# Narrower unused products in front of a retention, and one more unit's rows turned by VectorE

## The chip, the cores and the metric
The kernel runs on one core of one Trainium2 chip. The time is that of one execution on the device in microseconds (us), as the median of several runs. A profile is one execution, recorded by the hardware; its span goes from the first to the last instruction of the program and is a little shorter than the time of the same execution.

## The reference
Two stages follow each other. The first is a retention over 4 batches, 8 heads, 768 tokens and 64 features, a decaying sum over earlier tokens; the second sends every token to one of 8 experts and runs that expert's two products.

```
for t in range(S):
    state = gamma * state + k[:, :, t] (outer) v[:, :, t]
    y[:, :, t] = scale * q[:, :, t] . state
x = y, as 3072 tokens of 512 features
logits = x @ w_gate                       # 8 experts
in falling order of logits: token -> expert, at most 384 tokens each
out[tokens of e] = relu(x[tokens of e] @ w1[e]) @ w2[e]
```

The second stage can only begin when the logits of all tokens are known, since the assignment goes over all of them in falling order.

## The kernel before
The retention works on 24 units, one for each batch and each chunk of 128 tokens (unit u is batch u % 4, chunk u // 4). For a unit, TensorE makes the scores (line 409), VectorE multiplies them by a table of decays (line 412), TensorE multiplies them by the values (line 466), adds what the state gives (line 445) and adds to the state (line 481); ScalarE copies the result to the tile ys. After each chunk, `gate` makes the logits of its four units (line 562) and VectorE turns them. Units 0 to 3 are groups of their own, the others go in pairs; the last group is units 22 and 23. The order of TensorE, SyncE (SP), VectorE and ScalarE is written out by hand and is the order of the code.

In front of the retention and within its first steps stand products that nobody reads: `busy` (line 425) multiplies a tile of zeros by a tile of zeros, 12 times before the tables of decays, 8 times after them and 4 times after the first unit's scores. Each is 256 columns wide, and each makes two TensorE records, a weight load and a product.

The result of a unit has the tokens along the columns, and the second stage gathers rows of x from DRAM (the tensor xs). So every unit is turned, in one of two ways. Units 0 to 16 (`TURNED = 17`) are turned by VectorE in blocks of 32 x 32 (`block_rows`, line 510, into tiles x2 and x1) and written by four transfers on SP's queue for each unit or pair of units (`send`, line 526). Units 17 to 23 are left for the end: a generator, `rows_left`, turns one after the other by TensorE against an identity, two transposes for each half step (line 492), ScalarE copies the unit to xr (lines 502 and 504) and SP writes it by one transfer (line 506). The generator is advanced once, then three times, around the last gate and the last counts:

```
        while len(written) < TURNED:
            block_rows(len(written))
        for i in range(B * LONG, TURNED):
            send_one(i)
...
        rows = rows_left(left_over)
        next(rows)
...
        for _ in range(3):
            next(rows)
```

and then, with `STEPS = 7, 3, 0`, seven and three times between steps of `search`, which finds the tokens of the first expert: counts of tokens over a grid of thresholds (TensorE) are compared (VectorE, tile sg), spread over all partitions by a product with ones (TensorE, psm), and reduced (VectorE, nmb); this happens twice for the first expert, and the choice of the expert, the slots and the row numbers (idx) follow from it. A small memset on GpSimd (POOL, line 1267) waits until all rows of x are in DRAM; after it POOL issues the gathers of x (line 1118). The calls of the generator beyond its end do nothing.

The results ys of units before `TURNED` share 9 buffers; those of later units have a tile each. Tile x1, for units from 16 to `TURNED` - 1, has `TURNED` - 16 buffers.

Of the kernel before, what the change touches and what calls it, by code (L numbers as in the profile page):

```python
# [37 lines left out]
TURN = 42  # L38
QUIET = 2
PRESS = 16  # L40
WARM = (12, 8, 4)
PARTS = 3
KNOWN = 3
ROWBUFS = 5
LONG = 4
TURNED = 17
GUESS = 4
WINDOW = 6
ABOVE = 4
# [20 lines left out]
def tile_retention_moe(ctx: ExitStack, tc: tile.TileContext, qkv, wg, w1, w2,  # L70
# [74 lines left out]
    class Clock:  # L145

        pe = dve = pool = dma = 0
        busy, kept = [], []
# [133 lines left out]
    def prep_tiles():  # L282
        return (sw.tile([128, COLS], F32, name="m", bufs=2), sw.tile([128, COLS], BF, name="a", bufs=2),
                sw.tile([128, COLS, E], BF, name="oh", bufs=2),
                sw.tile([128, COLS, 64], BF, name="cmp", bufs=2))
# [93 lines left out]
    def decays():  # L379

        for s in range(2):
            ps = bank()
            nc.tensor.matmul(ps.rearrange("p a b -> p (a b)"), dp[:, s, 0:C], dp[:, s, C:], start=True, stop=True)
            nc.vector.tensor_tensor(dm[:, s], ps, up[:, None, :].to_broadcast([128, HP, C]), op=OP.mult)
        ps = bank()
        nc.tensor.matmul(ps.rearrange("p a b -> p (a b)"), qp[:, 0:128], qp[:, 128:], start=True, stop=True)
        nc.scalar.activation(qtb, ps, AF.Copy)

    def bank():
        return rp.tile([128, HP, C], F32, name="sc", bufs=4)  # L390
# [6 lines left out]
    def scores(us):  # L397

        c = units[us[0]][1]
        for u in us:  # L400
            if u == B + 1:
                gate(0)()
                states([B])
            k_, q_ = LD[u][:, 0], LD[u][:, 1]
            sc = [bank() for _ in range(2)]
            for pr in range(HP):
                for s in range(2):
                    r, w = slice(64 * s, 64 * s + 64), slice(pr * C, pr * C + C)
                    nc.tensor.matmul(sc[s][:, pr, :], k_[r, w], q_[r, w], start=True, stop=True)  # L409
            am = rw.tile([128, 2, HP, C], F32, name="am", bufs=4)  # L410
            for s in range(2):
                masked.append(nc.vector.tensor_tensor(am[:, s], sc[s], dm[:, s], op=OP.mult))  # L412
            qs = ks = None
            if c:
                qs = rw.tile([128, HP, C], F32, name="qs", bufs=4)
                if u == B:
                    ks = grown(u, c)
                scaled = nc.gpsimd.tensor_tensor(qs, q_.rearrange("p (a b) -> p a b", a=HP), qtb, op=OP.mult)
                if u == nu - 1:
                    gone.append(scaled)  # L420
            if c < NC - 1 and ks is None:
                ks = grown(u, c)
            st[u] = am, qs, ks

    def busy(k, o):
        for _ in range(k):
            nc.tensor.matmul(o, warm[:, 0:128], warm[:, 0:o.shape[1]], start=True, stop=True, skip_group_check=True)  # L427
# [3 lines left out]
    def outputs(us):  # L431

        c = units[us[0]][1]
        halved = us[-1] == nu - 1
        for u in us:
            yps[u] = [rp.tile([128, HP, C], F32, name="yp", bufs=2)]
        for u in us:
            yps[u] += [bank() if halved else yps[u][0]]
        if c:
            for pr in range(HP):  # L440
                for u in us:
                    b = units[u][0]
                    for s in range(2):
                        o = 64 * (s ^ b % 2)
                        nc.tensor.matmul(yps[u][pr // 2][o:o + 64, pr, :], T[b // 2][64 * s:64 * s + 64, b % 2, pr, :],  # L445
                                         st[u][1][64 * s:64 * s + 64, pr, :],
                                         start=(pr == 0 or halved and pr == 2), stop=False, skip_group_check=True)
# [4 lines left out]
    def mix(us):  # L452
# [3 lines left out]
        for u in us:  # L456
            b = units[u][0]
            YS[b, c] = (yk.tile([128, HP, C], F32, name=f"ys{b}_{c}") if b + B * c >= TURNED else
                        yk.tile([128, HP, C], F32, name="ys", bufs=9))
# [50 lines left out]
    def block_rows(i):  # L510
# [6 lines left out]
        else:  # L517
            x = x1[i] = rw.tile([128, 4, HP, 32], F32, name="x1", bufs=TURNED - B * LONG)
        nc.vector.transpose(x.rearrange("p t d r -> p d t r"), YS[b, c].rearrange("p d (t r) -> p d t r", t=4))
# [14 lines left out]
    def go(sends, k=None):  # L534
        for _ in sends:
            k = k and k - 1
            if k == 0:
                break
# [34 lines left out]
    st = {}  # L573

    wp = rp.tile([128, 512], F32, name="sc", bufs=4)
    busy(WARM[0], wp[:, 0:256])
    m0, a0, oh0, cmp0 = prep_tiles()
    parts, whole, ended, th0, turned = None, [], None, None, None
    groups = [[u] for u in range(B)] + [[u, u + 1] for u in range(B, nu, 2)]
# [46 lines left out]

    with tc.manual_schedule(engines={nc.vector.engine, nc.scalar.engine}):
        decays()
        busy(WARM[1], wp[:, 0:256])
        scores([0])  # L630
        for g, us in enumerate(groups):
            ahead = groups[g + 1] if g + 1 < len(groups) else ()
            if not g:
                busy(WARM[2], bank()[:, 0:2].rearrange("p a b -> p (a b)"))
            if g == LATER[-1] + 1:
                outputs(us)
                scores(ahead[:1])
                mix(us[:1])
                scores(ahead[1:])
            elif ahead and g not in LATER:  # L640
                scores(ahead)
            while spare:
                load(spare.pop(), masked[-4])
                if g >= EARLY:
                    go(sent, 6)
            if g == B:
                ended = 0
            if g != LATER[-1] + 1:
                outputs(us)
            if g > B:  # L650
                aside()
            if g == len(groups) - 1:
                mix(us)
            else:
                for u in us:
                    if u in yps:
                        mix([u])
                    if u == us[0] and g == len(groups) - 2:
                        guess()
                    if u != B:  # L660
                        states([u])
            if g == len(groups) - 2:
                guessed()
            if ahead and g in LATER:
                scores(ahead)
            for i, u in enumerate(us):
                if u + DEEP < nu:
                    if i and g >= EVEN:
                        spare.append(u + DEEP)
                    else:  # L670
                        load(u + DEEP)
                        if g >= EARLY:
                            go(sent, 5)
            if g > B:
                b1, c1 = units[groups[g - 1][-1]]
                if b1 == B - 1:
                    turned, ended = gate(c1), c1
            for k in range(BLOCKS.get(g, 0)):
                if k == 2 and turned:
                    turned = turned() and None  # L680
                block_rows(len(written))
            if turned:
                turned = turned() and None
            if g > B:
                next(chosen, None)
            if g == SEND:
                go(sent)
                go(send_two(2))
        last = gate(NC - 1)
        pc = rp.tile([128, 2 * E], F32, name="sc", bufs=4)  # L690
        early = [b * NC + c for c in (0, 2) for b in range(B)]
        for k, c in enumerate(early):
            by_two(pc, cmp0, oh0, c, k == 0, k == len(early) - 1)
# [4 lines that stand above are left out]
        left_over = [lambda i: rp.tile([128, DM], F32, name="yp", bufs=2)]  # L698
        rows = rows_left(left_over)
        next(rows)  # L700
        c = NC - 1
        last()
        cols = slice(c, COLS, NC)
        f = best(L[:, :, c], cols, m0, oh0)
        reach(cols, B, m0, cmp0, th0)
        f()
        n0 = other_half(pc, nc.vector)
        far = steps_above(m0)
        next(far)
        for _ in range(3):  # L710
            next(rows)
        for k in (NC - 2, c):
            for b in range(B):
                te.matmul(pc[0:64, 0:E], cmp0[:, b * NC + k, :], oh0[:, b * NC + k, :], start=False, stop=True,
                          skip_group_check=True)
        full(pc, n0, sgs[0])
        next(far)
        codes(cols, oh0, a0)
# [833 lines left out]
```

## Time and profile before

| | |
|---|---|
| median of 3 runs | 396.56 us (396.11 to 398.07) |
| the profiled execution | 396.47 us, its span 394.6 us |
| TensorE products (PE) | busy 385.6 us, 98% of the span |
| TensorE weight loads (PEld) | 337.4 us, 85% |
| VectorE (DVE) | 263.8 us, 67% |
| ScalarE (ACT) | 155.5 us, 39% |
| GpSimd (POOL) | 146.6 us, 37% |

Times in the rows are us from the start of the span unless they are marked ns; the first number of a row of the timeline is a start, the second the time from there to the end of the last of its instructions. PE are products and PEld weight loads, which overlap them. In brackets stands how long the engine was idle before the first of them and what ended that; "issue" means that it waited for nothing that the profile shows. A product's time goes on after the next one has started.

### The profile page before, as it was taken

What the parts mean: (1) busy time and instruction counts of PE and PEld (TensorE: products, weight loads), DVE (VectorE), ACT (ScalarE), POOL (GpSimd) and SP (SyncE); (2) the same over time, 40 slices, a digit from 0 to 9 for tenths busy, and PEclk for the clock granted to TensorE, in tenths of its full rate; (3) what the DMA queues carried; (4) which work ended last, traced back from release to release, by engine and by line L of the source; (5) the groups of instructions that cost most, each with busy time, mean ns of one, the idle gap of its engine ahead of it and who ended that gap; (6) DMA issues with size and microseconds to landing.
All of it is one profiled execution on the core that took longest, in us unless ns stands there. A gap on an engine that the chain in (4) does not pass through costs nothing.

```text
span 394.6 us, 8484 instructions
## 1 busy us (share of the span) xinstructions
PE 385.6 (98%) x3454; PEld 337.4 (85%) x3456; DVE 263.8 (67%) x639; ACT 155.5 (39%) x282; POOL 146.6 (37%) x166
## 2 busy tenths in 40 slices
PE   8999999998999999999999999999999999999994
PEld 5899999884998899789988987897799889889983
DVE  1449878977998588759868776787687167156300
ACT  1332324242661364056234524343363265156210
POOL 4489693204311620451253332153264137021011
PEclk9999999999999999999999999999999999999998
DMA  7999999948642662392385491365157215710001
GB/s 308 422 417 419 409 352 318 259 120 292 220 149 108 215 243 86 102 321 81 112 260 215 143 339 53 138 218 209 50 173 277 110 54 195 311 55 27 2 27 60
DMA packets 22862, 77.64 MB, mean 197 GB/s; under 512 B 2684, under 2 KB 11644, under 8 KB 16160
## 3 DMA queue, kind: packets, MB, share of 16 engines
q0 software_dynamic: 8448, 46.14, 33.2%
q1 hardware_dynamic: 14368, 30.88, 21.5%
q8 instruction: 29, 0.48, 0.5%
q14 instruction: 17, 0.14, 0.1%
HBM read 64.43 MB, written 12.58 MB: 195 GB/s over the span
## 4 chain that ended last, share of the span: by engine, by line
PE 78%; issue 12%; DVE 2%; POOL 2%; DMA 2%; ACT 1%; POOLq 1%; another core or an unknown queue 0%; ACTq 0%; DVEq 0%
PE py L1220 26%; PE ph L1181 25%; PE sc L409 7%; PE yp L466 6%; PE yp L445 3%; PE TP L481 2%; PE pt L1131 2%; PE psm L169 2%; PE sc L562 2%; PE sc L427 1%; DMA xg<-xs,idx 1%; POOL wraw L1071 1%; DMA out<-yo,oix 1%; POOL out L1201 1%; PE ph L1160 1%
## 5 line engine op out<-in xcount | busy, mean ns | idle before, releaser
L1181 PE MATMUL ph<-xh,w1h 128*128 128x384 f32 x248 | 81.7, 343 | 0.0
L1181 PE MATMUL ph<-xlo,w1h 128*128 128x384 f32 x256 | 81.6, 335 | 0.0
L1181 PE MATMUL ph<-xh,w1l 128*128 128x384 f32 x256 | 81.4, 335 | 0.0
L1220 PE MATMUL py<-w2h,hh 128*128 128x512 f32 x184 | 75.3, 409 | 0.0
L1220 PE MATMUL py<-w2h,hl 128*128 128x512 f32 x184 | 72.1, 392 | 0.0
L1220 PE MATMUL py<-w2l,hh 128*128 128x512 f32 x184 | 72.1, 392 | 0.0
L1201 POOL DMA_INDIRECT out<-yo,oix x23 | 27.9, 1214 | 105.5 <-ACT yo L1197 98.9
L1071 POOL DMA_INDIRECT wraw<-w,wix x32 | 38.3, 1197 | 58.1 <-DVE un L169 44.0
L1186 ACT ACTIVATE hh<-ph 128x384 fp32r<-128x384 f32 x64 | 31.4, 490 | 62.2 <-PE ph L1181 61.6
L169 DVE TENSOR_TENSOR w1l<-wraw,w1h 128x1024 fp32r<-128x1024 f32 (+1 forms) x36 | 39.2, 1101 | 14.4 <-ACT w1h L1104 14.4
L169 DVE SCALAR_TENSOR_TENSOR hl<-ph,hh 128x384 fp32r<-128x384 f32 x64 | 34.8, 553 | 19.3 <-ACT hh L1186 18.8
L1181 PEld LDWEIGHTS ph<-xlo,w1h 128*128 128x128 f32 x256 | 47.7, 188 | 0.0
L1181 PEld LDWEIGHTS ph<-xh,w1l 128*128 128x128 f32 x256 | 47.6, 188 | 0.0
L1181 PEld LDWEIGHTS ph<-xh,w1h 128*128 128x128 f32 x248 | 46.4, 188 | 1.1 <-ACT xh L1136 0.4
L1118 POOL DMA_INDIRECT xg<-xs,idx x24 | 28.7, 1194 | 40.1 <-issue 31.0
L1220 PEld LDWEIGHTS py<-w2h,hl 128*128 128x128 f32 x184 | 34.5, 188 | 7.5
L412 DVE TENSOR_TENSOR am<-sc,dm 128x512 f32<-128x512 f32 x48 | 30.0, 682 | 15.8 <-PE sc L409 15.8
L169 DVE TENSOR_TENSOR w2l<-wraw,w2h 128x1024 fp32r<-128x1024 f32 x32 | 38.6, 1218 | 2.3 <-ACT w2h L1104 2.3
L1220 PEld LDWEIGHTS py<-w2l,hh 128*128 128x128 f32 x184 | 34.7, 188 | 6.2 <-DVE w2l L169 0.6
L1220 PEld LDWEIGHTS py<-w2h,hh 128*128 128x128 f32 x184 | 34.7, 188 | 5.6
L1197 ACT ACTIVATE yo<-py 128x512 f32<-128x512 f32 x23 | 13.8, 598 | 58.6 <-PE py L1220 43.4
L1104 ACT ACTIVATE w1h<-wraw 128x1024 fp32r<-128x1024 f32 (+1 forms) x36 | 33.6, 957 | 6.1 <-DMA wraw<-w,wix 5.9
(194 smaller groups left out, 546.3 us busy)
## 6 DMA issues: line engine op xcount, KB each, us to landing
ld<-qkv SPq DMA_DIRECT2D x20, 1024.0 KB, 12.9
xs<-x SPq DMA_DIRECT2D x32, 128.0 KB, 5.0
ld<-qkv SPq DMA_DIRECT2D x4, 768.0 KB, 6.5
xs<-xr SPq DMA_DIRECT2D x7, 256.0 KB, 2.2
wraw<-w,wix POOLq DMA_INDIRECT x32, 6.8
xg<-xs,idx POOLq DMA_INDIRECT x24, 3.7
out<-yo,oix POOLq DMA_INDIRECT x23, 3.1
xs<-x SPq DMA_DIRECT2D x4, 64.0 KB, 2.3
```

What stands on the lines that cost most here:

```text
L169: return f(o, *a, **k)
L409: nc.tensor.matmul(sc[s][:, pr, :], k_[r, w], q_[r, w], start=True, stop=True)
L412: masked.append(nc.vector.tensor_tensor(am[:, s], sc[s], dm[:, s], op=OP.mult))
L466: nc.tensor.matmul(yp[o:o + 64, pr, :], values(u)[:, 2 * pr + s, :], st[u][0][:, s, pr, :], start=(not c and pr == 0), stop=(pr == p[1] - ...
L1071: nc.gpsimd.indirect_dma_start(out=t, out_offset=None, in_=w1v if nm == "w1" else w2v, in_offset=bass.IndirectOffsetOnAxis(ap=wix[:, hf:hf ...
L1104: nc.scalar.activation(p[0], p[2], AF.Copy)
L1118: nc.gpsimd.indirect_dma_start(out=t, out_offset=None, in_=xs, in_offset=bass.IndirectOffsetOnAxis(ap=found[n][0][:, j:j + 1], axis=0))
L1181: nc.tensor.matmul(ph, a[:, o:o + 128], x_[:, d], start=(k == 0 and not begun), stop=(k == len(prods) - 1), skip_group_check=begun)
L1186: nc.scalar.activation(hh[:, f], ph, AF.Relu)
L1197: nc.scalar.activation(yo, py, AF.Copy)
L1201: sct = nc.gpsimd.indirect_dma_start(out=out, out_offset=bass.IndirectOffsetOnAxis(ap=oix[:, j:j + 1], axis=0), in_=yo, in_offset=None, bo ...
L1220: nc.tensor.matmul(py, h_[:, f, t], a[:, o:o + DM], start=(k == 0), stop=(k == 23))
```

## The change
The three groups of unused products become 64 products of 48 columns, 32 of 64 and 16 of 64, in the same places, and `TURNED` goes from 17 to 18: unit 17 is turned by VectorE right after the groups' loop, by the `while` loop quoted above, and sent by four transfers behind those of unit 16; the generator begins with unit 18. Unit 17's result moves from a tile of its own to the 9 shared buffers, and x1 has two buffers. `STEPS` stays.

```diff
-WARM = (12, 8, 4)
+WARM = (64, 32, 16)
...
-TURNED = 17
+TURNED = 18
...
-    busy(WARM[0], wp[:, 0:256])
+    busy(WARM[0], wp[:, 0:48])
...
-        busy(WARM[1], wp[:, 0:256])
+        busy(WARM[1], wp[:, 0:64])
...
-                busy(WARM[2], bank()[:, 0:2].rearrange("p a b -> p (a b)"))
+                busy(WARM[2], bank()[:, 0, 0:64])
```

## Rows read from the trace of the kernel before

**Rows 1.** Windows: stage, its us, busy us and instructions per engine, PEclk, DMA, GB/s.
```profile
20.00:88.00 68.00, 67.54 (x1464) 61.49 (x1461) 54.76 (x135) 23.78 (x67) 39.37 (x35) 1.00 0.93 328
...
104.00:389.00 285.00, 284.73 (x1651) 251.81 (x1651) 188.92 (x442) 119.18 (x190) 91.08 (x98) 1.00 0.43 152
```

**Rows 2.** Timeline of all engines, front: start, us, engine, line, instruction, count, idle before.
```profile
1.12 2.74 PE L427 MATMUL sc<-warm 128*128 128x256 bf16 x12 [1.12 <-DVE warm L350]
...
3.79 0.13 PEld L383 LDWEIGHTS <-am 36*128 36x128 bf16 x2 [0.41 <-DMA am<-dparts]
...
5.30 1.89 PE L427 MATMUL sc<-warm 128*128 128x256 bf16 x8
...
7.24 2.08 PE L409 MATMUL sc<-ld 64*128 64x128 f32 x16
...
9.25 1.04 PE L427 MATMUL sc<-warm 128*128 128x256 bf16 x4
...
10.35 1.16 PE L409 MATMUL sc<-ld 64*128 64x128 f32 x16
```

**Rows 3.** Line 427, the unused products: ns of one instruction, min/median/max, first and last start.
```profile
L427 PEld LDWEIGHTS <-warm x24: 102/151/152, 1.1 to 9.7; 128*128 128x128 bf16 x24
```

**Rows 4.** Timeline, the early counts of the search.
```profile
84.70 0.36 PE L169 MATMUL sc<-oh,cmp 128*128 128x16 bf16 x8
```

**Rows 5.** Timeline, weight loads of one unit's products with the values.
```profile
70.72 0.85 PEld L466 LDWEIGHTS yp<-am,ld 128*64 128x64 f32 x15
...
72.02 0.13 PEld L466 LDWEIGHTS yp<-am,ld 128*64 128x64 f32 x1 [0.46 <-issue]
```

**Rows 6.** The page: engines' busy time and instructions, and the queue of instructions.
```profile
PE 385.6 (98%) x3454; PEld 337.4 (85%) x3456; DVE 263.8 (67%) x639; ACT 155.5 (39%) x282; POOL 146.6 (37%) x166
...
q8 instruction: 29, 0.48, 0.5%
```

**Rows 7.** Windows, the stretch that ends at the gap; columns as in rows 1.
```profile
67.20:72.02 4.82, 4.61 (x93) 3.87 (x81) 4.42 (x11) 0.51 (x2) 1.63 (x2) 1.00 1.01 350
```

**Rows 8.** Timeline, VectorE around the last logits.
```profile
83.67 0.41 DVE L169 TENSOR_TENSOR cmp<-m,th 128x256 bf16<-128x256 f32 x1
...
84.80 0.32 DVE L564 STREAM_TRANSPOSE L<-sc 128x128 f32<-128x128 f32 x1 [0.72 <-PE sc L562]
```

**Rows 9.** Line 519, the block transposes: ns of one, min/median/max.
```profile
L519 DVE STREAM_TRANSPOSE x<-ys x17: 656/673/702, 30.3 to 82.0; 128x512 f32<-128x512 f32 x17
```

**Rows 10.** Timeline, the first expert's search: sg, its spreading product, transposes of rows.
```profile
86.37 0.16 DVE L169 SCALAR_TENSOR_TENSOR sg<-sc,ng 64x8 bf16<-64x8 f32 x1
...
86.58 0.17 PE L169 MATMUL psm<-sg,onesb 128*128 128x8 bf16 x1 [0.25 <-DVE sg L169]
...
88.79 0.44 PE L492 MATMUL ph<-ident,ys 128*128 128x128 f32 x2
88.90 0.16 DVE L169 SCALAR_TENSOR_TENSOR sg<-psm,ng 64x8 bf16<-64x8 f32 x1
...
89.07 0.60 PE L492 MATMUL py<-ident,ys 128*128 128x128 f32 x4
...
89.50 0.17 PE L169 MATMUL psm<-sg,onesb 128*128 128x8 bf16 x1
```

**Rows 11.** Timeline, SP's transfers of x, and POOL before the first gather.
```profile
78.02 7.38 SPq L526 DMA_DIRECT2D xs<-x  x6
...
86.27 4.54 SPq L506 DMA_DIRECT2D xs<-xr  x7
...
93.25 0.09 POOL L1267 MEMSET spacer<- 1x1 f32 x1 [0.80 <-PE pt L169]
...
94.49 0.95 POOL L1118 DMA_INDIRECT xg<-xs,idx  x1 [1.16 <-DVE idx L169]
```

**Rows 12.** Line 526, the sends: ns that one takes SP, min/median/max.
```profile
L526 SPq DMA_DIRECT2D xs<-x x36: 303/476/1571, 50.0 to 84.9; - x36
```

## The prediction
> **What bounds the kernel now.** I read three views in this order: the busy times by stage, the order of instructions at both ends of the retention, and the idle times before single instructions. By stage, TensorE has work for 67.54 of the 68.00 us between 20 and 88 us and for 284.73 of the 285.00 us from 104 us on [rows 1]. So nothing but TensorE's own order sets the time there, except on the short bridge between them, 88 to 104 us, where a chain of small VectorE and TensorE steps finds the first expert's tokens. A microsecond taken off the front, out of the retention, or off that bridge therefore comes off the end one for one, and a change to VectorE, ScalarE or a queue elsewhere is worth nothing. The change touches exactly these three places, so I cost each by itself.
>
> **The front.** Here the reader is to see how long the unused products last and what waits behind them. Twelve of 256 columns take 2.74 us and eight take 1.89 us [rows 2], so four more cost 0.85 us, 212 ns each, which is 256 columns at 1.2 GHz. The granted-clock column reads 1.00 in the stages [rows 1], but this front runs at the lower level: sixteen score products take 2.08 us at 7.24 us and 1.16 us at 10.35 us [rows 2], so the clock rises between those two groups. The change keeps the columns (12 x 256 = 64 x 48, 8 x 256 = 32 x 64, 4 x 256 = 16 x 64) and cuts them into 88 more products, each a weight load and a product: 176 records. If columns are what they cost, a pair of 48 columns takes 40 ns and one of 64 takes 53 ns, and the three stretches stay as long as they are. What could be dearer is the pair itself. The trace has no narrow pair at the lower clock. The nearest row is eight pairs of 16 columns with the same 128 x 128 bf16 weights, 0.36 us [rows 4]; one alone takes 0.17 us [rows 10], so seven more cost 0.19 us, 27 ns each at 2.4 GHz and, if all of it goes with the clock, 54 ns at 1.2 GHz. That is the upper bound: 64 x 54 = 3.5 us from 1.12 us on, an end at 4.6 us where the decay products' first weight load now starts at 3.79 us, when their table has landed (it waited 0.41 us for that transfer [rows 2]). That would be 0.8 us late, of which some 0.3 us comes back because less work is left for the lower clock; the two 64-column stretches stay at 53 ns. So 0 to 0.5 us; I take 0, because at 212 ns the weight load of a product is wholly hidden behind the one before it, and 40 ns is still more than the 27 ns that a load and a product need together where their cost is seen.
>
> The Trainium skill, "TensorE: Matmul & The Clock Gate", section "LDWEIGHTS (loading the stationary operand)", has a rule against this: a weight load takes its number of columns over 1.2, which for 128 columns is an estimate of 107 ns, and then 64 + 32 + 16 narrow products would last some 6.9 us longer than now. The row of eight pairs in 0.36 us [rows 4] contradicts it for these weights, at the higher clock.
>
> **The retention.** At 72.02 us a weight load that waits for nothing starts after 0.46 us of idle time ended by "issue", in the middle of sixteen equal products of which fifteen have just gone through in one run [rows 5]. Nothing else stops TensorE like that between 20 and 88 us (0.46 us is about all that is missing there, 68.00 - 67.54 [rows 1]). What it lacked can only be its next instruction. Instructions come by their own queue, 29 packets and 0.48 MB, 16.6 KB each; TensorE alone has 3454 + 3456 records [rows 6], so if all the packets were its own, one would hold some 240 of them, and the gap looks like the place where a packet came late, while the DMA engines were busy for a share of 1.01 of the time before it [rows 7]. With 176 records more in front, the same packet boundary falls 176 records earlier: the stretch from 67.20 to 72.02 us holds 93 + 81 = 174 of them [rows 7], so near 67 us, and the next one some 60 records (240 - 176) later than the old place. Bounds: the gap vanishes, -0.46 us, or one like it arises at another boundary, 0. A third case, two gaps, would be +0.46. I take -0.40: between 20 and 88 us there are 1464 + 1461 records [rows 1], some twelve boundaries with one gap, so a shifted row of boundaries has most likely none (and 0.06 us of the idle time may be something else).
>
> The Trainium skill, "Runtime: NRT & Kernel Launch", section "Instruction fetch mechanics", says that instructions arrive in blocks of 256, the next block while the current one executes, so that crossing into one is mostly hidden. By that the shift would be worth nothing and the sum would be 0.40 us higher; the gap at 72.02 us says that here one crossing was not hidden.
>
> **The bridge.** What is removed: unit 17's four transposes on TensorE, its two copies on ScalarE and one 256 KB transfer. What is added: one 32 x 32 block transpose on VectorE and four transfers of 64 KB on SP's queue.
> VectorE: the block transpose takes 0.67 us in the median of seventeen (0.70 at most) [rows 9]. It comes after the compare that ends at 83.67 + 0.41 = 84.08 us and before the transpose of the last logits at 84.80 us, before which VectorE now sits idle for 0.72 us waiting for TensorE's gate products [rows 8]. It fits: 0 to 0.05 us late; without that cover it would cost its 0.70 us. I take 0.02, and drop it in rounding.
> TensorE: the row generator is called 1 + 3 times, then 7 and 3 times between steps of the search. Seven units need fourteen half-steps of two transposes, six need twelve. Up to the second step eleven calls are made in both kernels, so nothing changes there; in the three calls after it the old kernel still has three halves (2 + 4 transposes at 88.79 and 89.07 us) and the new one has one. Behind them waits the product that spreads the count: VectorE's sg is ready at 88.90 + 0.16 = 89.06 us, yet the product starts at 89.50 us [rows 10]. The same hand-over one stage earlier takes 0.05 us, from 86.37 + 0.16 = 86.53 to 86.58 us [rows 10]. So the product can start at about 89.12 us: -0.38 us. Bounds: -0.39 (sg + 0.05) and 0 (some other wait is just behind). From there to the first gather everything hangs on this product (VectorE's next reduction, the choice of expert, the slots, the indices), so what is late next is only the xs rows.
> SP: its sends end at 78.02 + 7.38 = 85.40 us, the seven row transfers are issued from 86.27 to 90.81 us [rows 11]. Four sends at 0.476 us (median [rows 12]) hold SP until some 87.3 us, so the first of the six row transfers is issued about 1 us later than the first of the seven now; SP catches up, because it takes the rows at ScalarE's pace (4.54 / 7 = 0.65 us each [rows 11]) and the last now comes one such step earlier. POOL's little memset, which waits for all rows to have landed, runs at 93.25 us, and then POOL idles 1.16 us until the indices come at 94.49 us [rows 11]. If the rows came more than 1.16 us late they would decide. I take 0.
>
> **Sum.** 396.47 (the profiled execution: a span of 394.6 and 1.9 around it) + 0 (front) - 0.40 (gap) - 0.38 (bridge) = 395.7 us. That execution is 0.09 us below the median of the three runs shown, so I say 395.8 us for a median. Half a per cent is 2.0 us, about what a measurement of this kernel can tell from no change.
>
> **Rivals.**
> (a) The gap stays or finds another boundary: only the bridge counts, 396.1 us. For it: the DMA engines' share is 0.93 over the whole stretch from 20 to 88 us [rows 1], so other boundaries meet traffic as dense as this one. Chance 0.25. (The section of the Trainium skill named above comes to the same time, by another way: no crossing costs anything, so none can be saved.)
> (b) Slower: the narrow products are bound by the pair, not by columns. Place: the 64 products from 1.12 us. The point from which it decides: with p ns a pair the decays start 64p - 2670 ns late; about half is given back by the rising clock, and above 53 ns the other 48 products add p - 53 each. At 60 ns this is (1.17 + 0.34) / 2 = 0.75 us, which cancels the gain; at 75 ns (2.13 + 1.06) / 2 = 1.6 us, so 397.3 us. For it: a weight load of the unused products lasts 151 ns in the median [rows 3]; against it: those loads are hidden now, and 27 ns for a whole pair is seen at the other level. Chance 0.10.
> (c) More products in the same columns bring the higher clock earlier. The first sixteen scores would take 1.16 instead of 2.08 us and the four products before the second group 0.5 instead of 1.04 us [rows 2]: -1.4 us, 394.3 us. Chance 0.07. The reverse, the second group of scores at the lower clock too (+0.92 us) and about as much again for the rest of its unit, gives 397.6 us, and with the next unit more; chance 0.05.
> (d) The block transpose or the rows of x become the wait in front of the first gather, and the bridge gains nothing: 396.1 us or a little more. Chance 0.03.
> The forecast itself, both gains within 0.3 us: 0.50.
>
> **Numbers.** Forecast and (a) lie between 395.4 and 396.5 us and hold 0.75; with (d) and about half of (b) the range to 397.3 us holds over 0.8. I set the lower end at 394.6 us, for the case that the clock rises a part of that stretch earlier. Faster by over 0.5% (below 394.6) is (c): 0.08. Slower by over 0.5% (above 398.5) is its reverse and the far end of (b): 0.05. The rest, 0.87, can hardly be told from no change.
>
> **What the changed profile would show.** Front: 64 products in about 2.7 us from 1.12 us, the second scores still near 10.35 us. Retention: no idle weight load ended by "issue" near 72 us, or a new one elsewhere. Bridge: a block transpose just ahead of the last logits, the spreading product some 0.05 us after sg, the first gather of x about 0.8 us earlier. I would be wrong if the scores start later than 10.9 us, if the gap is merely elsewhere, or if the product behind sg still waits.

## The result and the profile after

The changed kernel takes 400.26 us (median of 6 runs, 399.56 to 400.58) where the kernel before, on the same chip, takes 397.5 us (6 runs). The ratio is 1.0058, 95% interval 1.0032 to 1.0083: slower by 2.3 us going by the ratio and by 2.8 us going by the medians, where 395.8 us and no measurable difference were forecast. (This ratio and those of the experiments are estimates over all runs; they are not the quotients of the two medians.) The profiled execution took 400.49 us, its span is 398.8 us.

First the retention, by windows of the changed kernel (columns as in rows 1). The first row is the stretch of [rows 1]; the other four run from one stall, found below, to the next.

```profile
20.00:88.00 68.00, 66.29 (x1432) 59.64 (x1429) 54.22 (x126) 21.60 (x59) 39.22 (x34) 1.00 0.94 324
33.48:45.76 12.27, 12.27 (x252) 10.79 (x251) 10.46 (x20) 2.33 (x7) 10.06 (x10) 1.00 1.01 417
45.76:57.90 12.14, 11.74 (x254) 10.91 (x253) 9.29 (x18) 4.50 (x12) 8.79 (x8) 1.00 0.98 340
57.90:69.44 11.54, 11.28 (x253) 10.16 (x253) 9.40 (x21) 4.50 (x12) 5.93 (x5) 1.00 0.99 291
69.44:76.26 6.82, 6.33 (x126) 5.69 (x126) 6.07 (x16) 1.20 (x3) 1.93 (x3) 1.00 0.97 303
```

Before, 0.46 us of TensorE's time was missing between 20 and 88 us [rows 1]; now it is 68.00 - 66.29 = 1.71 us. In that stretch 32 products fewer have started. The granted clock is 1.00 in both.

Where it is missing shows in the timeline of TensorE's weight loads. Five times a load that waits for no other engine starts late ("issue"); such a late start in the middle of equal work is called a stall here:

```profile
33.49 1.52 PEld L409 LDWEIGHTS sc<-ld 64*128 64x128 f32 x25 [0.74 <-issue]
...
45.76 0.74 PEld L466 LDWEIGHTS yp<-am,ld 128*64 128x64 f32 x13 [0.21 <-issue]
...
57.91 0.18 PEld L409 LDWEIGHTS sc<-ld 64*128 64x128 f32 x1 [0.61 <-issue]
...
69.45 0.15 PEld L562 LDWEIGHTS sc<-ys,wgf 128*32 128x32 f32 x5 [0.53 <-issue]
...
76.27 0.36 PEld L481 LDWEIGHTS TP<-ld 128*64 128x64 f32 x9 [0.63 <-issue]
```

They are of one kind with the gap of [rows 5], and they sit in the middle of equal work, as that one did. (Idle times of 0.17 to 0.20 us also stand at some first loads of a batch of products in both kernels, and are not meant.) The windows tell the spacing: from one to the next TensorE starts 252 + 251 = 503, 507, 506 and 252 weight loads and products. That is two blocks, two, two and one of some 252. Before 33.49 us the trace holds 601 products, 602 loads and 13 semaphore instructions, 1216 in all; counted in this way, every stall named here and in the experiments stands in front of record 193 + 256 n, and the gap of before in front of record 2753 = 193 + 256 x 10. So the blocks hold 256 instructions of TensorE, and they are the packets of the instruction queue: queue q8 moves packets of 16 KB, and from 20 to 88 us one of them starts between each two neighbouring records of this series. The first record of a block is called a boundary below.

The five idle times add up to 2.72 us. The early counts of the search started at 84.70 us [rows 4]; in a second profile of before (experiment 8) at 84.56 us; here at 87.32 us, 2.76 us after the latter. That the two sums agree so closely is partly chance. Set product by product against that second profile, the changed kernel falls back by 0.7, 0.2, 0.7, 0.5 and 0.7 us at the five places and hardly anywhere else, until it is 3.3 us behind; near 79 us, where the kernel before waits for VectorE for 0.29 us (line 616), 0.6 us of it come back. So the retention's loss is the stalls.

The front of the changed kernel, TensorE's timeline:

```profile
1.12 2.74 PE L427 MATMUL sc<-warm 128*128 128x48 bf16 x64 [1.12 <-DVE warm L350]
...
5.30 1.89 PE L427 MATMUL sc<-warm 128*128 128x64 bf16 x32
7.24 1.85 PE L409 MATMUL sc<-ld 64*128 64x128 f32 x16
9.02 0.64 PE L427 MATMUL sc<-warm 128*128 128x64 bf16 x16
9.59 1.28 PE L409 MATMUL sc<-ld 64*128 64x128 f32 x16
```

64 products of 48 columns last the same 2.74 us as twelve of 256, 32 of 64 the same 1.89 us [rows 2]: columns set the time. Here the clock rose within the first scores (1.85 instead of 2.08 us), so the second scores begin 0.76 us earlier than in [rows 2]. That moment moves by itself: with the same front, experiment 1 had its sixteen 64-column products in 1.04 us, all at the lower level, and a second profile of before had its second scores at 9.90 us. It is worth little here, since the third unit's scores then wait for their load (0.4 us in this profile, 1.1 us in a second one of this kernel); they start at 12.59 us, where the second profile of before has them at 12.48 us.

The bridge, all engines:

```profile
86.62 0.70 DVE L519 STREAM_TRANSPOSE x<-ys 128x512 f32<-128x512 f32 x1
87.32 0.36 PE L169 MATMUL sc<-oh,cmp 128*128 128x16 bf16 x8
87.42 0.32 DVE L564 STREAM_TRANSPOSE L<-sc 128x128 f32<-128x128 f32 x1
...
90.64 3.21 SPq L506 DMA_DIRECT2D xs<-xr  x6
...
91.52 0.16 DVE L169 SCALAR_TENSOR_TENSOR sg<-psm,ng 64x8 bf16<-64x8 f32 x1
...
91.73 0.17 PE L169 MATMUL psm<-sg,onesb 128*128 128x8 bf16 x1
...
97.41 0.09 POOL L1267 MEMSET spacer<- 1x1 f32 x1 [2.76 <-DMA xs<-xr]
98.09 0.94 POOL L1118 DMA_INDIRECT xg<-xs,idx  x1 [0.59 <-DVE lim L169]
...
104.70 0.63 PE L1131 MATMUL py<-ident,xg 128*128 128x128 f32 x4 [0.19 <-DMA xg<-xs,idx]
```

The block transpose ends at 87.32 us and the last logits are turned at 87.42 us without a wait. The product that spreads sg starts 0.05 us after it (91.52 + 0.16 = 91.68). From the early counts to this product it is 91.73 - 87.32 = 4.41 us, where it was 89.50 - 84.70 = 4.80 us [rows 4, 10]: -0.39 us, as forecast. But the rows of x came late. SP's sends last until 90.5 us, its first row transfer is issued at 90.64 us, 1.1 us ahead of the spreading product and no longer 3.2 us ahead [rows 10, 11]; one of unit 17's four sends, at 87.70 us, holds SP for 1.87 us, where the forecast took the median of 0.48 us for each [rows 12]; POOL's memset waits for the rows (2.76 us) and the gather for the memset. The third tile of x, which is turned last, waits for its gather.

### The profile page after: what moved, and what is told of

The parts are those of the page before. It is cut to its first block, busy times and chain, and to the rows that moved or that the text cites. A ratio compares the mean times of both kernels' runs of the same rounds, so it can differ in the third digit from the quotient of the medians.

```text
span 398.8 us, 8653 instructions
## 1 busy us (share of the span) xinstructions
PE 386.9 (97%) x3538; PEld 339.5 (85%) x3540; DVE 265.9 (67%) x640; ACT 154.6 (39%) x280; POOL 144.8 (36%) x166
## 4 chain that ended last, share of the span: by engine, by line
PE 73%; issue 13%; DMA 5%; DVE 3%; POOL 3%; ACT 1%; POOLq 1%; SPq 0%; another core or an unknown queue 0%; DVEq 0%
PE py L1220 25%; PE ph L1181 24%; PE sc L409 6%; PE yp L466 5%; PE yp L445 2%; DMA ld<-qkv 2%; PE TP L481 2%; PE psm L169 2%; PE pt L1131 2%; PE sc L562 2%; POOL wraw L1071 1%; DMA out<-yo,oix 1%; DMA xg<-xs,idx 1%; DVE w1l L169 1%; POOL out L1201 1%
## 5 line engine op out<-in xcount | busy, mean ns | idle before, releaser
L1201 POOL DMA_INDIRECT out<-yo,oix x23 | 26.1, 1136 | 107.6 <-ACT yo L1197 100.8
L1071 POOL DMA_INDIRECT wraw<-w,wix x32 | 37.3, 1164 | 57.4 <-DVE un L169 43.3
L1118 POOL DMA_INDIRECT xg<-xs,idx x24 | 29.8, 1240 | 39.6 <-issue 31.0
```

What stands on the lines that cost most here:

```text
L1071: nc.gpsimd.indirect_dma_start(out=t, out_offset=None, in_=w1v if nm == "w1" else w2v, in_offset=bass.IndirectOffsetOnAxis(ap=wix[:, hf:hf ...
L1118: nc.gpsimd.indirect_dma_start(out=t, out_offset=None, in_=xs, in_offset=bass.IndirectOffsetOnAxis(ap=found[n][0][:, j:j + 1], axis=0))
L1201: sct = nc.gpsimd.indirect_dma_start(out=out, out_offset=bass.IndirectOffsetOnAxis(ap=oix[:, j:j + 1], axis=0), in_=yo, in_offset=None, bo ...
```

## The experiments

All but experiments 5 and 8, which are one execution each, are timed beside the kernel before on the same chip. "Records" are TensorE records more in front than in the kernel before.

**1. The records alone.**

```diff
-WARM = (12, 8, 4)
+WARM = (64, 32, 16)
-    busy(WARM[0], wp[:, 0:256])
+    busy(WARM[0], wp[:, 0:48])
...
```

> Only the unused products are changed (64 of 48 columns, 32 of 64, 16 of 64), unit 17 stays with TensorE. Theory A, the place of the packets of instructions: the 176 records move every 256-record boundary of TensorE's stream to a worse place between the loads, so most of the loss is here: gaps of 0.4 to 0.8 us in front of the records 1217, 2241, 2753 and 3009 as in the changed kernel, +2 to +3 us. Theory B, unit 17's transfers in front of the first gather: these are not here, so the time is that of the kernel before, 0 to +0.5 us.

398.98 us against 397.91 us, ratio 1.0021 (0.9995 to 1.0046): by time alone this is not clear of no change. Its profile has five stalls:

```profile
33.89 1.52 PEld L409 LDWEIGHTS sc<-ld 64*128 64x128 f32 x25 [0.73 <-issue]
...
46.73 0.74 PEld L466 LDWEIGHTS yp<-am,ld 128*64 128x64 f32 x13 [0.67 <-issue]
...
58.60 0.18 PEld L409 LDWEIGHTS sc<-ld 64*128 64x128 f32 x1 [0.34 <-issue]
...
64.85 0.30 PEld L409 LDWEIGHTS sc<-ld 64*128 64x128 f32 x3 [0.33 <-issue]
...
76.51 0.37 PEld L481 LDWEIGHTS TP<-ld 128*64 128x64 f32 x9 [0.32 <-issue]
```

They stand in front of records 1217, 1729, 2241, 2497 and 3009. Three of the four that were expected are among them; record 2753 has none, and 1729 and 2497 are new. The stalls come with the records, not with unit 17.

**2. Unit 17 alone.**

```diff
-TURNED = 17
+TURNED = 18
```

> Only unit 17 is turned by VectorE, the unused products are those of before. Theory A: gaps as in the kernel before (one, near 72 us), time -0.4 to +0.4 us, because the 0.4 us that the search gains is lost again while the first gather waits for the rows of x. Theory B: the rows of x cost most of the loss, +1.5 us or more.

397.95 us against 397.91 us, 0.9996 (0.9974 to 1.0019): no difference. The profile has none of the stalls.

**3 and 4. A whole block of 256 records in front, without and with unit 17 on VectorE.** If it is the place of the boundaries that counts, 256 records put each boundary back to where it was.

```diff
-WARM = (12, 8, 4)
+WARM = (88, 40, 24)
-    busy(WARM[0], wp[:, 0:256])
+    busy(WARM[0], wp[:, 0:35])
-        busy(WARM[1], wp[:, 0:256])
+        busy(WARM[1], wp[:, 0:51])
-                busy(WARM[2], bank()[:, 0:2].rearrange("p a b -> p (a b)"))
+                busy(WARM[2], bank()[:, 0, 0:43])
```

> The unused products become 88 of 35 columns, 40 of 51 and 24 of 43: 256 records more than before in the same columns, and unit 17 stays with TensorE. Theory A: the boundaries fall where they fell before, so the gaps and the time of the kernel before come back, within 0.5 us. Theory C, more and narrower products in front cost time by themselves (in the front, or by more records): at least as slow as with 176 records, +2 us or more.

> The changed kernel with 80 records more in the same columns (88 of 35, 40 of 51, 24 of 43), so 256 more than before, unit 17 turned by VectorE. Theory A: as the kernel with unit 17 alone, -0.4 to +0.4 us against before. Theory C: as slow as the changed kernel or slower, +2.3 us or more.

398.45 us (1.0016, 0.9996 to 1.0036) and 398.03 us (0.9994, 0.9973 to 1.0016) against 397.91 us. TensorE is busy for 67.75 and 67.41 us of the 68.00 us between 20 and 88 us, and neither has one of the stalls of experiment 1. More and still narrower products, and none of the stalls; but the intervals of experiments 1 and 3 overlap, so by time this was not settled yet.

**5. The changed kernel without its late loads** (those of units 16 to 23 are left out; these units work on what is in the buffer). One execution; its results are not those of the task.

```diff
         c = units[u][1]
+        if u >= 2 * DEEP:
+            LD[u] = LD[u - DEEP]
+            if u == nu - 1:
+                nc.sync.dma_start(ti, thr)
+            return
```

> The changed kernel without the loads of units 16 to 23: these units take the data of units 8 to 15, so results and time are not those of the task; it is run for its gaps. If a packet of instructions comes late because it queues behind the loads of q, k and v, the gaps in front of records 1729, 2241, 2753 and 3009 (0.24, 0.69, 0.53 and 0.71 us in the changed kernel's profile), after about 45 us, vanish, and the one in front of record 1217 at 33 us stays. If the gaps have nothing to do with the loads (a fixed cost of a boundary, the sequencer), they all stay.

396.47 us, where the kernel before took 397.6 us in one execution on the same chip and the changed kernel 400.49 us in its profiled one. Windows of this run:

```profile
20.00:50.00 30.00, 29.57 (x628) 26.76 (x624) 23.48 (x44) 9.62 (x29) 27.82 (x25) 1.00 0.99 375
50.00:88.00 38.00, 37.75 (x832) 34.38 (x829) 33.78 (x94) 13.59 (x35) 11.20 (x10) 1.00 0.44 95
```

Up to 50 us, with the DMA engines at 0.99, there is one stall, at 45 us (a load of line 466's products, 0.67 us late at 45.36 us, against 0.21 us in the changed kernel). The expectation missed on both places there: the stall at 33 us was to stay, but record 1217 starts at 32.52 us without one, and the one at 45 us was to go. After 50 us, with 95 GB/s instead of 255, none is left: the boundaries are the same ones, at about 57, 63, 68, 74 and 80 us, and nothing waits at them. So in this execution the stalls end where the loads end, and not every boundary under the loads has one.

**6 and 7. Part of the records, 64 and 128.**

```diff
-WARM = (12, 8, 4)
+WARM = (28, 18, 10)
-    busy(WARM[0], wp[:, 0:256])
+    busy(WARM[0], wp[:, 0:110])
...
```

For 128 records it is (48, 26, 14), with 64, 79 and 73 columns; with 64 records 110, 114 and 102.

> Only the unused products: 28 of 110 columns, 18 of 114, 10 of 102, so 64 records more than before in the same columns, unit 17 with TensorE. Theory A (the place of the boundaries between the loads decides): gaps in front of records 193 + 256 n for some n and nowhere else, their sum between 0 and 3 us, the time over that of before by about that sum. Theory C (cost grows with the count of records) is already weak; it would give a third of what 176 records cost, +0.4 to +0.9 us, without gaps at these records.

> As the last, with 48 products of 64 columns, 26 of 79 and 14 of 73: 128 records more than before. Theory A: gaps in front of records 193 + 256 n only; half a block from before and only 48 records from 176, so nearer to the 176 records: +1 to +3 us. Theory C: two thirds of what 176 records cost, without such gaps.

398.51 us (1.0021, 1.0001 to 1.0042) and 397.71 us (1.002, 0.9996 to 1.0045) against 397.39 us. One of the ten executions with 64 records took 759.85 us, for a reason that is not known; it is not in the ratio. With 64 records two loads are late by issue (0.24 us at 29.74 and 0.27 us at 48.17 us), with 128 three (0.49 us at 34.66, 0.32 at 46.92, 0.35 at 58.46 us). The stalls grow from 0.5 to 1.2 us and then, with 176, to 2.7 us; the times of these two can hardly be told apart from before, and with 128 the loss of 1 to 3 us that was expected did not come. Its profile shows why: the early counts start at 85.90 us, 1.34 us after those of the second profile of before, but from there to the turn of the third tile of x it takes 16.36 us and not 17.33 us, so 1 us comes back (see "What stays open").

**8. The kernel before, a second profile.**

> The kernel before once more, for a second profile: which of the steps in which the first profile differs from the others come and go without any change. I expect the front (when the clock rises) and the late step near 204 us to differ from the first profile by up to 0.8 us each, and no more than one gap of over 0.3 us between 20 and 80 us.

397.6 us. The place of [rows 5] in this execution, and the rows of the bridge:

```profile
70.55 0.85 PEld L466 LDWEIGHTS yp<-am,ld 128*64 128x64 f32 x16
...
84.56 0.36 PE L169 MATMUL sc<-oh,cmp 128*128 128x16 bf16 x8
...
89.37 0.17 PE L169 MATMUL psm<-sg,onesb 128*128 128x8 bf16 x1
...
101.89 0.63 PE L1131 MATMUL py<-ident,xg 128*128 128x128 f32 x4
```

The sixteen loads go through in one run. The gap that the forecast meant to save is not in every execution of the kernel before. Nor did it cost much where it was: product by product, the first profile is 0.2 us behind this one ahead of the gap, 0.65 us behind it after the gap, and 0.1 us behind at 79.5 us, since this one waits there (0.29 us, line 616). This profile is also 0.6 us longer from about 204 us on, as those of the changed kernel and of all the experiments are; only the first one of before is short there. It is therefore the better one to compare with.

**9 to 12. All on one chip:** the changed kernel again, experiment 4 again, the changed kernel with 432 records (176 + 256, so its boundaries fall where those of 176 do), experiment 1 again. The edit of the third:

```diff
-WARM = (64, 32, 16)
+WARM = (120, 72, 48)
-    busy(WARM[0], wp[:, 0:48])
+    busy(WARM[0], wp[:, 0:26])
-        busy(WARM[1], wp[:, 0:64])
+        busy(WARM[1], wp[:, 0:28])
-                busy(WARM[2], bank()[:, 0, 0:64])
+                busy(WARM[2], bank()[:, 0, 0:21])
```

> The changed kernel itself, beside the others on one chip. If the loss comes from the stalls of TensorE in front of every 256th of its records (records number 193 + 256 n), it is again some 2 us above before, about 400 us, with several idle times ended by issue of 0.2 to 0.8 us between 30 and 80 us. If that one profile was a chance and the change costs nothing, it lies within 0.8 us of before.

> The changed kernel with 256 records more in front instead of 176. By the stalls: the same time as before within 0.5 us, so about 2 us below the changed kernel on the same chip, and no stall over 0.3 us. If instead narrower unused products or unit 17 on VectorE cost the time, it is as slow as the changed kernel or slower.

> The changed kernel with 432 records more in front (176 + 256) in the same 6144 columns. If only the place of every 256th record counts, it is the changed kernel's phase again: stalls in front of the same products as in the changed kernel, and some 2 us above the kernel with 256 records, near 400 us. If the loss grew with the number of records, it is beyond the changed kernel by another 2 us or more; if the phase does not count, it is like the kernel with 256 records.

> The 176 records alone, unit 17 as before. By the stalls: within 0.6 us of the changed kernel on the same chip, some 1.5 to 2.5 us above before. If unit 17's rows on VectorE cost a part of the loss (late row transfers in front of the first gather), it is 1 us or more below the changed kernel.

| on one chip, before 397.7 us | records | unit 17 | us | ratio (interval) |
|---|---|---|---|---|
| changed kernel again | 176 | VectorE | 400.17 | 1.0047 (1.0026 to 1.0068) |
| experiment 4 again | 256 | VectorE | 398.26 | 1.0001 (0.9977 to 1.0024) |
| 432 records | 432 | VectorE | 401.33 | 1.0070 (1.0049 to 1.009) |
| experiment 1 again | 176 | TensorE | 399.38 | 1.0030 (1.0007 to 1.0053) |

Twelve runs each: the changed kernel lies between 399.50 and 401.33 us, the one with 256 records between 397.11 and 399.02 us in eleven, with one at 401.02 us. The loss comes with 176, goes with 256 and comes again with 432, and the intervals of the changed kernel and of 432 lie above that of 256. Neither the number of the records nor the width of the products can do that; the place of the boundaries can. The late weight loads of the changed kernel's second profile:

```profile
39.41 0.63 PEld L466 LDWEIGHTS yp<-am,ld 128*64 128x64 f32 x12 [0.25 <-issue]
...
45.84 0.74 PEld L466 LDWEIGHTS yp<-am,ld 128*64 128x64 f32 x13 [0.94 <-issue]
...
57.72 0.18 PEld L409 LDWEIGHTS sc<-ld 64*128 64x128 f32 x1 [0.34 <-issue]
...
75.51 0.36 PEld L481 LDWEIGHTS TP<-ld 128*64 128x64 f32 x9 [0.61 <-issue]
```

and of the kernel with 432 records, where the second and the third stand in front of the same products as 33.49 and 57.91 us above:

```profile
28.94 1.41 PEld L409 LDWEIGHTS sc<-ld 64*128 64x128 f32 x23 [0.41 <-issue]
35.49 1.52 PEld L409 LDWEIGHTS sc<-ld 64*128 64x128 f32 x25 [0.64 <-issue]
...
60.18 0.18 PEld L409 LDWEIGHTS sc<-ld 64*128 64x128 f32 x1 [1.16 <-issue]
```

Which boundaries of the family are late differs a little from one execution to the next. They sum to 2.14 us and 2.21 us. The early counts start at 86.56 us in the former, 2.00 us after the second profile of before. In the latter they start at 88.66 us, 4.10 us after it, and that takes a second cause. It shows in its front, TensorE's timeline:

```profile
1.12 3.38 PE L427 MATMUL sc<-warm 128*128 128x26 bf16 x120 [1.12 <-DVE warm L350]
4.43 1.03 PE L383 MATMUL sc<-am 36*128 36x512 bf16 x2
...
8.09 1.23 PE L409 MATMUL sc<-ld 64*128 64x128 f32 x8
```

120 pairs take 3.38 us, 28 ns each, where 26 columns would take 22 ns at 1.2 GHz: here the pair sets the time, the decays start 0.63 us late and the first scores 0.85 us late [rows 2]. That is rival (b), at a width that the change does not reach. By the third unit's scores it is 1.34 us (13.96 against 12.62 us in the changed kernel's second profile), and the measured times differ by 401.33 - 400.17 = 1.16 us.

The profile of experiment 12 is of an execution of 401.78 us, above its median. It has stalls of 0.73 us at 35.92, 0.61 us at 60.07 and 1.15 us at 67.13 us, and 2.0 us more in its front: TensorE is busy for 0.72 us between 5.30 and 7.24 us, because the first scores wait for their load, and then the granted clock is 0.52 between 7.24 and 9.00 us and 0.50 from there to 13.00 us, the lower level. The second scores wait 1.18 us for their load, start at 10.99 us, 1.1 us later than in the second profile of before, and take 2.08 us instead of 1.16 us. These 0.9 us are the reverse of rival (c), in one execution.

The windows of experiment 4's second run between 20 and 88 us (columns as in rows 1) are those of before:

```profile
20.00:88.00 68.00, 67.45 (x1466) 61.58 (x1463) 56.59 (x137) 23.94 (x67) 39.29 (x35) 1.00 0.94 328
```

and its bridge, all engines, keeps the gain for the first expert:

```profile
84.64 0.36 PE L169 MATMUL sc<-oh,cmp 128*128 128x16 bf16 x8
...
89.05 0.17 PE L169 MATMUL psm<-sg,onesb 128*128 128x8 bf16 x1
...
93.47 0.09 POOL L1267 MEMSET spacer<- 1x1 f32 x1 [1.50 <-PE psm L169]
94.15 0.94 POOL L1118 DMA_INDIRECT xg<-xs,idx  x1 [0.59 <-DVE et L169]
...
101.58 0.63 PE L1131 MATMUL py<-ident,xg 128*128 128x128 f32 x4
```

The early counts to the spreading product take 4.41 us, as in the changed kernel. From that product to the third tile's turn it is 12.53 us, as in the second profile of before (89.37 to 101.89 us: 12.52 us); in the changed kernel it is 104.70 - 91.73 = 12.97 us, and in its second profile 103.93 - 90.97 = 12.96 us. Further on this execution loses the gain again: 0.3 us ahead of the second profile of before at the third tile, it is 0.5 us behind from 147 us on. What takes this is open.

## Why the prediction was wrong

**The base, 396.47 us: about 1 us too low.** The shown runs lay low; in the later comparisons the kernel before has medians of 397.39 to 397.91 us in 19 to 35 runs.

**The retention, "I take -0.40": this step failed, by its sign and size.** Its mechanism was right: the gap is a late packet of instructions, and the records in front move the boundaries. Three things were wrong. "A shifted row of boundaries has most likely none" took one gap in twelve boundaries as a chance for each boundary by itself, with +0.46 us as the worst. Experiments 9 to 11 show that the boundaries are late together: their places are fixed by the number of records, and with 176 more four or five of them are late at once, 2.1 to 2.7 us in the changed kernel's two profiles. The gap at 72.02 us was one execution's, and most of it was made up for by 79.5 us, as experiment 8 shows; so what is taken out of the retention did not come off one for one. And "0.46 us is about all that is missing there" was a chance agreement of two numbers: at the gap the products were idle for 0.21 us only, and 0.25 us were lost at 86.58 us [rows 10]. The size of a block, "some 240" by the page's totals, is 256.

How near to the edge this runs shows when each boundary is set against the packet of the instruction queue that started last before it. From the trace's list of DMA packets and of TensorE's records in the changed kernel's first profile, in us:

```
record  starts  last packet started  between  idle before (issue)
1217    33.49   31.00                2.48     0.74
1473    40.01   37.59                2.42     none
1729    45.76   43.33                2.43     0.21
1985    51.60   48.65                2.96     0.17, as at this load in before
2241    57.91   55.64                2.27     0.61
2497    63.64   60.63                3.01     none
2753    69.45   67.19                2.25     0.53
3009    76.27   73.86                2.41     0.63
3265    82.28   78.87                3.42     none
```

A stall ends 2.25 to 2.48 us after the packet started, and where there were more than 2.5 us there is none; the gap of before ended 2.45 us after its packet. (In the other profiles stalls end 2.2 to 2.6 us after it. A boundary that comes so soon need not stall: the one at 40.01 us does not, and the second profile of before has three between 30 and 44 us, 2.40 to 2.47 us after their packets, with at most 0.11 us of idle time.) The packets themselves start 2.6 to 4.4 us after the boundary one block earlier (67.19 - 63.64 = 3.55, 73.86 - 69.45 = 4.41), and 1.1 to 3.8 us in the second profile of before. Without the late loads, from 52 us on in experiment 5, they start -0.4 to 0.9 us from it. Some 4.4 + 2.4 = 6.8 us from boundary to boundary is more than the 5.1 to 6.5 us that a block lasts here without a stall. The Trainium skill, "Runtime: NRT & Kernel Launch", section "Instruction fetch mechanics", has the blocks of 256 instructions right, but crossings as "mostly hidden"; here they cost 2.7 us in one execution. Why a packet waits longer at these boundaries than at those of the kernel before was not tried and stays open. That it queues behind a load issued shortly before is a guess that experiment 5 allows.

**The front, 0 us: right.** 64 products in 2.74 us, so rival (b) fell for 48 columns; its pair costs 28 ns at 1.2 GHz (experiment 11), about the 27 ns of the one estimate and not the 54 ns of the other. The estimate by the rule for weight loads of the Trainium skill, "TensorE: Matmul & The Clock Gate", section "LDWEIGHTS (loading the stationary operand)", 6.9 us more, did not come true. Rival (c) did happen in part, the second scores starting 0.76 us earlier in this profile, and was worth little, as the load of unit 2 was waited for next; the prediction had not asked what is late next there. Its reverse came in the profile of experiment 12, at 0.9 us.

**The bridge, -0.38 us: right for its step, and then taken back.** The step measured -0.38 to -0.40 us in every profile with unit 17 on VectorE. "SP: I take 0" was mis-sized by 0.4 us at the third tile. POOL's idle 1.16 us before the first gather was read as margin, but POOL needs 0.59 us from the memset's end to the gather in any case, so 93.34 + 0.59 = 93.93 against 94.49 us left 0.56 us. And SP was not 1 us later against the spreading product but 2.1 us, so that the first gather started 1.4 us later against it (98.09 - 91.73 = 6.36 us, before 4.99 us). With the retention undisturbed (experiment 10) SP is 1.9 us ahead of that product, the gather comes 0.1 us later against it than before, and the gain stays; in both profiles of the changed kernel it does not. That is rival (d) in its price, at +0.43 us. It is not the stalls by themselves: with 432 records there are stalls and a gather 1.0 us late against the product, and yet the third tile is turned 12.41 us after it (93.07 to 105.48 us). What also counts is how long the rows take from the third gather's start to that turn: 4.86 us in the second profile of before, 4.11 us in the changed kernel, 3.93 us with 432 records. Why this differs is open.

The sum of these against 395.8 us: 1 us of base, 0.4 us of gap not saved and 2.1 to 2.7 us of stalls, 0.4 us of bridge make 3.9 to 4.5 us; measured are 4.5 us.

**What stays open.** With 176 records, unit 17 on VectorE measured 400.17 and on TensorE 399.38 us; 0.6 us at most were expected, and the intervals overlap. The traces show where 0.8 us can come from: from the early counts to the turn of the third tile it takes 16.36 us in both profiles of the records alone (experiments 1 and 12) and with 128 records, but 17.38 and 17.36 us in the changed kernel and 17.33 to 17.36 us in the kernel before and in experiment 3. In the former the rows arrive sooner, 3.9 us from the third gather's start to the turn; the gather itself starts when it did before. So the kernel with the records alone has two effects against each other, stalls of 2.4 to 2.5 us and a bridge that is 1 us shorter, and the cause of the second is not known. And no version was found that beats the kernel before: the bridge's 0.39 us is too little to measure in 398 us.

## What to carry to other kernels

Where TensorE runs small products back to back and DMA is full, the number of instructions ahead of a stretch is a tuning knob in itself, modulo 256: before crediting or blaming an edit near the start, add unused instructions up to a whole block and time it again. An unexplained idle time by "issue" in the middle of equal work can be one of a family: look for the others 256 instructions apart, and take a second profile before counting on the one. Where a chain is shortened, measure the margin of the other inputs from the moment at which the consumer could have started, not from its idle time.

## What the runs showed of the hardware

Stalls of TensorE of 0.2 to 1.2 us in front of some of the instructions 193 + 256 n, while the DMA engines carry loads (share 0.97 to 1.02), and none with a share of 0.44 (experiment 5). Between 20 and 83 us no such instruction started less than 2.19 us after the start of the packet that belongs to it by their order, in any profile here. A pair of weight load (128 x 128, bf16) and product lasts as long as its columns at 48 columns (40 ns with the clock at 1.2 GHz: 2.74 us / 64 is 43 ns with the start) and 28 ns at 26 columns. From the end of GpSimd's small memset to the gather behind it it takes 0.59 us in all eight profiles in which the memset is what the gather comes after.
